# A gated feed-forward kernel: split value units in one PSUM bank in place of two, more of them, and row folds that add across the columns first

## The chip, the cores and the metric

The kernel runs on one core of a Trainium2 chip. The metric is the device time of one execution in microseconds (us). PSUM is the memory that matmuls write to; it is used here in 8 banks. Engine names: PE is the matmul engine (TensorE), PEld its weight loads, DVE is VectorE, ACT is ScalarE, POOL is GpSimd, SP issues DMAs. A profile shows one execution; its span is 1 to 3 us shorter than the time that is measured around it.

## The reference, cut to what matters

```python
def _attn_ref(x):                      # x: (8, 3008, 256)
    X = np.fft.fft(x, axis=1)
    X = np.fft.fft(X, axis=2)
    return X.real.astype(np.float32)

def _moe_ref(x, w_gate, w_val, w_out): # x: (24064, 256), d_ff 1536
    g = x @ w_gate
    silu = g * (1.0 / (1.0 + np.exp(-g)))
    val = x @ w_val
    return (silu * val @ w_out).astype(np.float32)
```

The kernel uses the symmetry of the transform. For each pair of output rows k and M-k it computes an even part P and an odd part Q. A row's value (or gate) is "even + odd", the mirrored row's is "even - odd". So one column of a tile serves two rows, called plus and minus below.

## The kernel before

Work goes through 24 tiles of at most 512 columns. A tile has 12 units, one for each 128 of the 1536 hidden features. A unit makes gate and value for plus and minus rows, and the two products `hp` and `hm`. Between the units run the output matmuls of the tile before (four at a time, 256 columns each), the row transforms of later rows (`L567`, `L543`), and on POOL the "folds", which prepare the coefficients of those transforms from the rows.

A plain unit needs six matmuls of 512 columns: plus gate (2), plus value (2), and one more on each to turn plus into minus. A split unit needs five: it takes the even and the odd part of the value apart, and DVE makes both combinations.

```python
psG = ...tile_pool(name="psG", bufs=3, PSUM)   # gate banks
psV = ...tile_pool(name="psV", bufs=3, PSUM)   # value banks
psO = ...tile_pool(name="psO", bufs=2, PSUM)   # output banks; 8 banks in all
...
SPLIT = (0, 2, 3, 5, 7, 9)                     # split units of a tile
SPLIT_END = (0, 1, 2, 4, 5, 7, 8, 10, 11)      # of the last two split tiles

def part_a(u):
    ...
    mm(g, Wp, 0, Pt, True, False)              # L716: all of mm()
    mm(g, Wq, 0, Qt, False, True)
    if split(u):
        e = psV.tile(...); mm(e, Wp, 1, Pt, True, True)     # even part, a bank
        o = psV.tile(...); mm(o, Wm, 1, Qt, True, True)     # odd part (times -2), another bank
        sg = Silu(g)                                        # ACT, L728
        es = bc[t] * w0[f] + e                              # DVE, L731
        vp = o * -0.5 + es                                  # DVE, L733
        vm[reversed] = o * 0.5 + es                         # DVE, L735
        hp[:, f] = sg * vp                                  # POOL, L736
        state[u] = (g, vm); return
    v = psV.tile(...); mm(v, Wp, 1, Pt, True, False); mm(v, Wq, 1, Qt, False, True)
    sg = Silu(g); hp[:, f] = sg * v                         # ACT L743, DVE L744
    state[u] = (g, v)

def part_b(u):                                 # one unit later
    g += Wm, Qt                                             # L753; for a plain unit v += Wm, Qt too
    if split(u):
        sg[reversed] = Silu(g); hm[:, f] = sg * v           # ACT L757, POOL L758
        return
    sg = Silu(g); hm[:, f][reversed] = sg * v               # ACT L761, DVE L762

# a fold, per 4 x 256 block of rows (on POOL)
tt(SDf[0], up, down, add); tt(SDf[1], up, down, subtract)   # L153, 1024 elements each
even: E = SDf[0] mirrored + SDf[0];  odd: O = SDf[1] mirrored - SDf[1]     # 512 each
...

for i, u in enumerate(units):                  # main loop, cut
    part_a(u); output matmuls x4; part_b(previous); output matmuls x4
    fold steps; row transforms in some units (after the fifth unit of a tile)
```

The code above is shortened (cuts are marked, calls are written as formulas). Tiles 0 to 2 and the last have no split units.

## Time and profile before

| | before |
|---|---|
| time, median of 4 | 688.56 us (687.79 to 689.6) |
| span of the profile | 685.5 us |
| PE, DVE, ACT, POOL busy | 672.8, 514.6, 432.9, 579.1 us |
| matmuls | 4374 |

The first two parts of the page below, and its chain, are of the kernel before: busy time of each engine with the share of the span and the number of instructions, then the chain of work that ended last.

```profile
PE 672.8 (98%) x4374; PEld 414.2 (60%) x4374; DVE 514.6 (75%) x919; ACT 432.9 (63%) x764; POOL 579.1 (84%) x565
...
PE 89%; DVE 5%; issue 2%; POOL 2%; ACT 0%; DVEq 0%; ACTq 0%; POOLq 0%
```

PE is the limit. The windows view of the kernel before says so for the main part; columns are the window, its length, busy time and number of instructions of PE, PEld, DVE, ACT and POOL, then clock, DMA share and GB/s.

```profile
250.00:350.00 100.00, 99.63 (x645) 61.09 (x643) 77.31 (x132) 63.78 (x111) 98.42 (x90) 1.00 0.30 81
350.00:450.00 100.00, 99.62 (x639) 59.74 (x637) 75.50 (x132) 62.69 (x110) 94.65 (x89) 1.00 0.23 59
```

POOL is nearly as busy as PE here.

The timeline of the kernel before shows that: start, duration, engine, line, operation. Units f=2 and f=3 of one tile, both split (some lines left out):

```profile
248.35 0.38 PE L716 MATMUL g<-Pt,Wp 128*128 128x512 bf16 x1
248.56 0.38 PE L716 MATMUL g<-Qt,Wq 128*128 128x512 bf16 x1
248.78 0.38 PE L716 MATMUL v<-Pt,Wp 128*128 128x512 bf16 x1
249.00 0.38 PE L716 MATMUL v<-Qt,Wm 128*128 128x512 bf16 x1
...
249.20 0.75 DVE L731 SCALAR_TENSOR_TENSOR es<-bc,w,v 128x512 f32<-128x512 f32 x1 [0.73 <-PE v L716]
...
250.68 0.68 DVE L735 SCALAR_TENSOR_TENSOR vv<-v,es 128x512 f32<-128x512 f32 x1
...
250.95 0.38 PE L716 MATMUL v<-Pt,Wp 128*128 128x512 bf16 x1
...
251.28 0.68 DVE L762 TENSOR_TENSOR hm<-sg,v 128x512 bf16<-128x512 f32 x1
...
251.42 0.38 PE L716 MATMUL v<-Qt,Wm 128*128 128x512 bf16 x1
251.64 0.60 PE L676 MATMUL o<-Wo,hp 128*128 128x256 bf16 x4
```

In the first unit matmuls of 512 columns start 0.21 to 0.22 us apart: that is what one costs when nothing waits. In the second, the odd part's matmul starts 0.47 us after the even part's, 0.26 us late. It starts 0.06 us after DVE has ended its read of the older odd part (250.68 + 0.68 = 251.36): it waits for the bank.

From the starts of all matmuls one can work out a "gap": the time to the next start, less columns/2.4 + 2.5 ns (215.8 ns for 512 columns, which fits undisturbed neighbours to about 1 ns). Summed over the run, matmuls at this price need 645.0 us, and the gaps after 25 us that matter are: 7.57 us before the value matmuls of units after 60 us (0.26 us each in most cases), and 13.22 us in the row transforms after 60 us.

### The profile page before, as it was taken

The page shows a single profiled execution, that of the slowest core. Times are in us where ns is not written, and L with a number is a line of the kernel's source. Part 1 is how long each engine was busy: PE and PEld are TensorE (multiplying, and loading weights), DVE is VectorE, ACT ScalarE, POOL GpSimd, SP SyncE. Part 2 cuts the span into 40 slices and gives each one's busy share as a digit, 9 for nine tenths or more (in the row PEclk, how much of TensorE's full clock was granted, in tenths as well). Part 3 has the DMA queues.
Part 4 walks back from the last instruction along what each step waited for, and adds up shares of the span by engine and source line. Part 5 has one row for each costly group of instructions (what it writes and reads, how often), then busy time and mean ns, then how long its engine had stood idle before and what let it go on. Part 6 is the DMA issues. An engine that isn't in the chain of part 4 may idle for free.

```text
span 685.5 us, 13259 instructions
## 1 busy us (share of the span) xinstructions
PE 672.8 (98%) x4374; PEld 414.2 (60%) x4374; DVE 514.6 (75%) x919; ACT 432.9 (63%) x764; POOL 579.1 (84%) x565
## 2 busy tenths in 40 slices
PE   8999999999999999999999999999999999999997
PEld 5446655666656566565665566655665656656676
DVE  8896667777777777777777777777786777788862
ACT  7676655666656666565666666655665656656663
POOL 8897987899998999999998989997999555658920
PEclk9999999999999999999999999999999999999999
DMA  9657353324315213335134111125111111101112
GB/s 220 115 77 133 102 138 113 96 76 101 99 32 134 67 51 105 86 71 131 41 76 116 48 32 47 47 58 128 46 48 32 38 40 33 47 31 47 47 48 70
DMA packets 45567, 52.55 MB, mean 77 GB/s; under 512 B 6290, under 2 KB 33466, under 8 KB 45498
## 3 DMA queue, kind: packets, MB, share of 16 engines
q1 hardware_dynamic: 42314, 49.35, 27.4%
q0 software_dynamic: 3184, 2.36, 2.7%
q8 instruction: 34, 0.56, 0.4%
q14 instruction: 35, 0.29, 0.2%
HBM read 29.39 MB, written 24.65 MB: 79 GB/s over the span
## 4 chain that ended last, share of the span: by engine, by line
PE 89%; DVE 5%; issue 2%; POOL 2%; ACT 0%; DVEq 0%; ACTq 0%; POOLq 0%
PE o L676 34%; PE v L716 17%; PE g L716 16%; PE g L753 9%; PE v L753 4%; PE g L567 3%; PE v L567 3%; DVE vv L735 3%; DVE vv L733 1%; PE v L543 1%; PE g L543 1%; PE g L856 1%; PE g L421 1%; PE v L421 1%; PE o L430 0%
## 5 line engine op out<-in xcount | busy, mean ns | idle before, releaser
L736 POOL TENSOR_TENSOR hp<-sgv,vv 128x512 bf16<-128x512 f32 (+1 forms) x126 | 160.1, 1272 | 54.3 <-DVE vv L733 42.4
L676 PE MATMUL o<-Wo,hp 128*128 128x256 bf16 (+2 forms) x1140 | 169.7, 273 | 0.0
L676 PE MATMUL o<-Wo,hm 128*128 128x256 bf16 (+2 forms) x1140 | 169.7, 273 | 0.0
L758 POOL TENSOR_TENSOR hm<-sgv,vv 128x512 bf16<-128x512 f32 (+1 forms) x126 | 159.6, 1272 | 8.5 <-ACT sgv L757 8.1
L676 PEld LDWEIGHTS <-hp 128*128 128x128 bf16 (+2 forms) x1140 | 111.9, 98 | 68.3 <-issue 7.8
L676 PEld LDWEIGHTS <-hm 128*128 128x128 bf16 (+2 forms) x1140 | 111.8, 98 | 64.8 <-issue 4.9
L744 DVE TENSOR_TENSOR hp<-sg,v 128x512 bf16<-128x512 f32 (+2 forms) x162 | 107.9, 666 | 33.2 <-ACT sg L743 32.4
L731 DVE SCALAR_TENSOR_TENSOR es<-bc,w,v 128x512 f32<-128x512 f32 (+1 forms) x126 | 93.7, 744 | 50.5 <-PE v L716 50.3
L762 DVE TENSOR_TENSOR hm<-sg,v 128x512 bf16<-128x512 f32 (+2 forms) x162 | 107.4, 663 | 24.1 <-ACT sg L761 14.4
L761 ACT ACTIVATE sg<-g 128x512 f32<-128x512 f32 (+2 forms) x162 | 94.7, 585 | 45.6 <-PE g L753 45.4
L743 ACT ACTIVATE sg<-g 128x512 f32<-128x512 f32 (+2 forms) x162 | 94.4, 583 | 45.0 <-PE g L716 43.5
L716 PE MATMUL g<-Qt,Wq 128*128 128x512 bf16 (+2 forms) x288 | 108.0, 375 | 0.5 <-DVE Qt L580 0.5
L716 PE MATMUL g<-Pt,Wp 128*128 128x512 bf16 (+2 forms) x288 | 108.1, 376 | 0.1
L716 PE MATMUL v<-Pt,Wp 128*128 128x512 bf16 (+2 forms) x288 | 108.0, 375 | 0.0
L753 PE MATMUL g<-Qt,Wm 128*128 128x512 bf16 (+2 forms) x288 | 108.0, 375 | 0.0
L757 ACT ACTIVATE sgv<-g 128x512 f32<-128x512 f32 (+1 forms) x126 | 75.3, 598 | 47.4 <-PE g L753 41.1
L728 ACT ACTIVATE sgv<-g 128x512 f32<-128x512 f32 (+1 forms) x126 | 75.1, 596 | 40.3 <-PE g L716 35.5
L733 DVE SCALAR_TENSOR_TENSOR vv<-v,es 128x512 f32<-128x512 f32 (+1 forms) x126 | 87.0, 690 | 17.6 <-PE v L753 1.0
L735 DVE SCALAR_TENSOR_TENSOR vv<-v,es 128x512 f32<-128x512 f32 (+1 forms) x126 | 85.7, 680 | 2.7 <-POOL hm L758 2.7
L716 PEld LDWEIGHTS <-Wp 128*128 128x128 bf16 x576 | 56.2, 98 | 41.0 <-issue 4.2
L682 ACT COPY ev<-o 128x512 f32<-128x512 f32 x90 | 52.7, 586 | 30.8 <-PE o L676 28.2
L153 POOL TENSOR_TENSOR SDf<-XA 128x1024 f32<-128x1024 f32 x28 | 66.0, 2364 | 5.2 <-DMA XC<-in_x_dram 3.3
(165 smaller groups left out, 738.0 us busy)
## 6 DMA issues: line engine op xcount, KB each, us to landing
out_dram<-ev SPq DMA_DIRECT2D x96, 128.0 KB
XA<-in_x_dram SPq DMA_DIRECT2D x32, 256.0 KB
XA<-in_x_dram SPq DMA_DIRECT2D x112, 64.0 KB
XC<-in_x_dram SPq DMA_DIRECT2D x32, 120.0 KB
XC<-in_x_dram SPq DMA_DIRECT2D x105, 32.0 KB
out_dram<-ev SPq DMA_DIRECT2D x12, 120.0 KB
out_dram<-ev SPq DMA_DIRECT2D x10, 112.0 KB
XA<-in_x_dram SPq DMA_DIRECT2D x1, 1024.0 KB
```

The costliest lines, as they stand in the source:

```text
L676: nc.tensor.matmul(ps[:n, j, :], hts[minus][:, f, c:c + n], Wo[:, f, :], start=(f == 0), stop=(f == nF - 1))
L716: nc.tensor.matmul(ps[:, :w], Wt[:, gv, fs], src[:, :w], start=start, stop=stop, skip_group_check=True)
L731: stt(es[:, :w], bc[t][:, :w], w0[:, f:f + 1], e[:, :w], op0=Alu.mult, op1=Alu.add)
L733: stt(vp[:, :w], o[:, :w], -0.5, es[:, :w], op0=Alu.mult, op1=Alu.add)
L735: stt(vm[:, w - 1::-1], o[:, :w], 0.5, es[:, :w], op0=Alu.mult, op1=Alu.add)
L736: nc.gpsimd.tensor_tensor(hts[t][0][:, f, :w], sg[:, :w], vp[:, :w], op=Alu.mult)
L743: nc.scalar.activation(sg[:, :w], g[:, :w], AF.Silu)
L744: nc.vector.tensor_tensor(hts[t][0][:, f, :w], sg[:, :w], v[:, :w], op=Alu.mult)
L753: nc.tensor.matmul(ps[:, :w], Wm[:, gv, f * P:(f + 1) * P], Qt[:, :w], start=False, stop=True, skip_group_check=True)
L758: nc.gpsimd.tensor_tensor(hts[t][1][:, f, :w], sg[:, :w], v[:, :w], op=Alu.mult)
L761: nc.scalar.activation(sg[:, :w], g[:, :w], AF.Silu)
L762: nc.vector.tensor_tensor(hts[t][1][:, f, w - 1::-1], sg[:, :w], v[:, :w], op=Alu.mult)
```

## The change

A split unit now starts its value with the even part alone in one bank. DVE reads it (`es`), and one unit later PE adds the odd part onto the same bank. Plus is then the bank itself, and minus is twice `es` less the bank. The plus product moves from POOL to DVE. There are more split units (8 of 12, in the last two split tiles 10). A fold adds one mirrored row block across the columns first, so that one sum of about 1024 elements takes the place of two.

```diff
-    SPLIT = (0, 2, 3, 5, 7, 9)
-    SPLIT_END = (0, 1, 2, 4, 5, 7, 8, 10, 11)
+    SPLIT = (0, 2, 3, 5, 6, 8, 9, 11)
+    SPLIT_END = (0, 1, 2, 3, 5, 6, 7, 8, 9, 11)
@@ part_a, split unit
-            e = psV.tile([P, T], F32, name="v")
-            mm(e, Wp, 1, Pt, True, True)
-            o = psV.tile([P, T], F32, name="v")
-            mm(o, Wm, 1, Qt, True, True)
...
+            v = psV.tile([P, T], F32, name="v")
+            mm(v, Wp, 1, Pt, True, False)
...            (silu of plus into sp, es as before from v)
-            stt(vp[:, :w], o[:, :w], -0.5, es[:, :w], op0=Alu.mult, op1=Alu.add)
-            stt(vm[:, w - 1::-1], o[:, :w], 0.5, es[:, :w], op0=Alu.mult, op1=Alu.add)
-            nc.gpsimd.tensor_tensor(hts[t][0][:, f, :w], sg[:, :w], vp[:, :w], op=Alu.mult)
+            state[u] = (g, v, sg, es)
@@ part_b, split unit
+            nc.tensor.matmul(v[:, :w], Wq[:, 1, fs], Qt[:, :w], start=False, stop=True, ...)
+            nc.vector.scalar_tensor_tensor(vm[:, w - 1::-1], es[:, :w], 2.0, v[:, :w],
+                                           op0=Alu.mult, op1=Alu.subtract)
+            nc.scalar.activation(sm[:, w - 1::-1], g[:, :w], AF.Silu)
+            nc.gpsimd.tensor_tensor(hts[t][1][:, f, :w], sm[:, :w], vm[:, :w], op=Alu.mult)
+            nc.vector.tensor_tensor(hts[t][0][:, f, :w], sp[:, :w], v[:, :w], op=Alu.mult)
@@ fold_steps
-            tt(SDf[r, a], X[r, 0:4, q, :], X[r, 7:3:-1, 1 - q, :], op=op)       # twice: add, subtract
+            tt(F[:, :, 1:D], up[:, :, 1:D], down[:, :, D - 1:0:-1], op=Alu.add) # once
+            tt(E[:, :, P:P + 1], up[:, :, 0:1], down[:, :, 0:1], op=Alu.add)    # 4 elements
...            (even and odd read F; 12 fold steps in place of 14; buffers: sp 3, sgv 3, es 3, vv 3)
```

Even with 38 more split units a split unit keeps its five matmuls, so only their number changes the count.

More of the change, by code (lines that the diff above doesn't have):

```diff
@@ L142, in load_c, with fold_steps, cross @@
                                      in_=rows_at(b, 0, [[R * D, 1], [R * D, 4], [1, D]]))])
-    def fold_steps(eng, X, CE, BB, q, r, given=None):
+    def fold_steps(eng, X, CE, BB, q, r):
         tt = eng.tensor_tensor
-        S, Dd = given or (SDf[r, 0], SDf[r, 1])
+        F = SDf[r, q]
         E, O = EOf[r, 0], EOf[r, 1]
-        def sd(a, op):
-            tt(SDf[r, a], X[r, 0:4, q, :], X[r, 7:3:-1, 1 - q, :], op=op)
+        up, down = X[r, 0:4, q], X[r, 7:3:-1, 1 - q]
+        def cross():
+            tt(F[:, :, 1:D], up[:, :, 1:D], down[:, :, D - 1:0:-1], op=Alu.add)
+            tt(E[:, :, P:P + 1], up[:, :, 0:1], down[:, :, 0:1], op=Alu.add)
         def even():
-            tt(E[:, :, 0:P], S[:, :, P:0:-1], S[:, :, P:D], op=Alu.add)
-            eng.tensor_copy(E[:, :, P:P + 1], S[:, :, 0:1])
+            tt(E[:, :, 0:P], F[:, :, P:0:-1], F[:, :, P:D], op=Alu.add)
         def odd():
-            tt(O[:, :, 0:P], Dd[:, :, P:0:-1], Dd[:, :, P:D], op=Alu.subtract)
+            tt(O[:, :, 0:P], F[:, :, P:0:-1], F[:, :, P:D], op=Alu.subtract)
         def ab():
@@ L169, in bb, with quarter_rows @@
         def bb():
-            tt(BB[r, q, 0], E[:, 0:4:3, 0:P], E[:, 2:0:-1, 0:P], op=Alu.subtract)
-            tt(BB[r, q, 1], O[:, 0:2, 0:P], O[:, 2:4, 0:P], op=Alu.subtract)
-            tt(BB[r, q, 1, :, 0:1], S[:, 3::-3, 0:1], S[:, 1:3, 0:1], op=Alu.subtract)
-        return [lambda: sd(0, Alu.add), lambda: sd(1, Alu.subtract), even, odd, ab, ce, bb]
+            quarter_rows(tt, E, O, BB[r, q])
+        return [cross, even, odd, ab, ce, bb]
+    def quarter_rows(tt, E, O, B_):
+        tt(B_[:, 0], E[:, 0:4:3, 0:P], E[:, 2:0:-1, 0:P], op=Alu.subtract)
+        tt(B_[:, 1], O[:, 0:2, 0:P], O[:, 2:4, 0:P], op=Alu.subtract)
+        tt(B_[:, 1, :, 0:1], E[:, 3::-3, P:P + 1], E[:, 1:3, P:P + 1], op=Alu.subtract)
     coefA, coefC = {}, {}
@@ L490 @@
     for q in range(2):
-        steps = fold_steps(nc.gpsimd, None, CEa, BBa, q, slice(0, P),
-                           given=(SA[:, 0, :, q, :], SA[:, 1, :, q, :]))
-        for i in (2, 3, 6):
-            steps[i]()
+        S, Dd = SA[:, 0, :, q, :], SA[:, 1, :, q, :]
+        E, O = EOf[:, 0], EOf[:, 1]
+        ptt(E[:, :, 0:P], S[:, :, P:0:-1], S[:, :, P:D], op=Alu.add)
+        nc.gpsimd.tensor_copy(E[:, :, P:P + 1], S[:, :, 0:1])
+        ptt(O[:, :, 0:P], Dd[:, :, P:0:-1], Dd[:, :, P:D], op=Alu.subtract)
+        quarter_rows(ptt, E, O, BBa[:, q])
     nc.gpsimd.dma_start(out=Wo, in_=moe_w_out.rearrange("(f p) d -> p f d", p=P))
@@ L616 @@
     sgp = ctx.enter_context(tc.tile_pool(name="sg", bufs=3))
-    sgv = ctx.enter_context(tc.tile_pool(name="sgv", bufs=4))
-    esp = ctx.enter_context(tc.tile_pool(name="es", bufs=2))
+    spp = ctx.enter_context(tc.tile_pool(name="sp", bufs=3))
+    sgv = ctx.enter_context(tc.tile_pool(name="sgv", bufs=3))
+    esp = ctx.enter_context(tc.tile_pool(name="es", bufs=3))
     bcp = ctx.enter_context(tc.tile_pool(name="bc", bufs=2))
-    vvp = ctx.enter_context(tc.tile_pool(name="vv", bufs=4))
+    vvp = ctx.enter_context(tc.tile_pool(name="vv", bufs=3))
     evp = ctx.enter_context(tc.tile_pool(name="evO", bufs=4))
@@ L722, in part_a @@
         if split(u):
-            e = psV.tile([P, T], F32, name="v")
-            mm(e, Wp, 1, Pt, True, True)
-            o = psV.tile([P, T], F32, name="v")
-            mm(o, Wm, 1, Qt, True, True)
-            sg = sgv.tile([P, T], F32, name="sgv")
+            v = psV.tile([P, T], F32, name="v")
+            mm(v, Wp, 1, Pt, True, False)
+            sg = spp.tile([P, T], F32, name="sp")
             nc.scalar.activation(sg[:, :w], g[:, :w], AF.Silu)
-            stt = nc.vector.scalar_tensor_tensor
             es = esp.tile([P, T], F32, name="es")
-            stt(es[:, :w], bc[t][:, :w], w0[:, f:f + 1], e[:, :w], op0=Alu.mult, op1=Alu.add)
-            vp = vvp.tile([P, T], F32, name="vv")
-            stt(vp[:, :w], o[:, :w], -0.5, es[:, :w], op0=Alu.mult, op1=Alu.add)
-            vm = vvp.tile([P, T], F32, name="vv")
-            stt(vm[:, w - 1::-1], o[:, :w], 0.5, es[:, :w], op0=Alu.mult, op1=Alu.add)
-            nc.gpsimd.tensor_tensor(hts[t][0][:, f, :w], sg[:, :w], vp[:, :w], op=Alu.mult)
-            state[u] = (g, vm)
+            nc.vector.scalar_tensor_tensor(es[:, :w], bc[t][:, :w], w0[:, f:f + 1], v[:, :w],
+                                           op0=Alu.mult, op1=Alu.add)
+            state[u] = (g, v, sg, es)
             return
@@ L750, in part_b @@
         Pt, Qt = pq_tiles(t)
-        g, v = state.pop(u)
-        for gv, ps in ((0, g), (1, v))[:1 if split(u) else 2]:
-            nc.tensor.matmul(ps[:, :w], Wm[:, gv, f * P:(f + 1) * P], Qt[:, :w], start=False, stop=True,
-                             skip_group_check=True)
-        if split(u):
-            sg = sgv.tile([P, T], F32, name="sgv")
-            nc.scalar.activation(sg[:, w - 1::-1], g[:, :w], AF.Silu)
-            nc.gpsimd.tensor_tensor(hts[t][1][:, f, :w], sg[:, :w], v[:, :w], op=Alu.mult)
+        g, v, *kept = state.pop(u)
+        fs = slice(f * P, (f + 1) * P)
+        nc.tensor.matmul(g[:, :w], Wm[:, 0, fs], Qt[:, :w], start=False, stop=True, skip_group_check=True)
+        if kept:
+            nc.tensor.matmul(v[:, :w], Wq[:, 1, fs], Qt[:, :w], start=False, stop=True, skip_group_check=True)
+            sp, es = kept
+            vm = vvp.tile([P, T], F32, name="vv")
+            nc.vector.scalar_tensor_tensor(vm[:, w - 1::-1], es[:, :w], 2.0, v[:, :w],
+                                           op0=Alu.mult, op1=Alu.subtract)
+            sm = sgv.tile([P, T], F32, name="sgv")
+            nc.scalar.activation(sm[:, w - 1::-1], g[:, :w], AF.Silu)
+            nc.gpsimd.tensor_tensor(hts[t][1][:, f, :w], sm[:, :w], vm[:, :w], op=Alu.mult)
+            nc.vector.tensor_tensor(hts[t][0][:, f, :w], sp[:, :w], v[:, :w], op=Alu.mult)
             return
+        nc.tensor.matmul(v[:, :w], Wm[:, 1, fs], Qt[:, :w], start=False, stop=True, skip_group_check=True)
         sg = sgp.tile([P, T], F32, name="sg")
@@ L771, in spread @@
         seq.extend((lo + (i * (hi - lo)) // (n - 1), what, i) for i in range(n))
-    spread(("C", 1), 14, 6, 14)
-    spread(("A", 1), 14, 15, 24)
+    spread(("C", 1), 12, 6, 14)
+    spread(("A", 1), 12, 15, 24)
     lo = 25
@@ L777 @@
         u = slot[(b, 0)] - 1
-        spread(("C", b), 14, lo, (lo + u) // 2)
-        spread(("A", b), 14, (lo + u) // 2 + 1, u)
+        spread(("C", b), 12, lo, (lo + u) // 2)
+        spread(("A", b), 12, (lo + u) // 2 + 1, u)
         lo = min(u + 26, slot[(b + 1, 0)] - 2)
-        spread(("A", b + 1), 14, u + 2, lo)
+        spread(("A", b + 1), 12, u + 2, lo)
         lo += 1
@@ L792, in fold_step @@
         kind, b = what
-        q, j = divmod(i, 7)
+        q, j = divmod(i, 6)
         if i == 0:
@@ L801, in fold_step @@
         queue[what].pop(0)()
-        if q == 1 and j == 1:
+        if q == 1 and j == 0:
             act_at.setdefault(max(unit + 2, 11), []).append(what)
```

## The prediction

> **What bounds the kernel.** TensorE. In the windows view it is busy 99.5 to 99.7% of the stretches from 150 to 550 us; DVE has 76%, POOL 84 to 98%. But busy time overstates a matmul: the groups give 375 ns for 512 columns, while in the PE timeline of an undisturbed stretch they start 0.215 us apart (300.27, 300.49, 300.70, 300.92), and the 256-column output matmuls 0.109 us. The Trainium skill says the same ("TensorE: Matmul & The Clock Gate", Back-to-back issue gap: columns/2.4 + 2.5 ns when warm). At this price all matmuls need 645 us of the 685.5 us span. About 36 us are extra gap: 13 us before 60 us, about 12 us in the row transforms, and 7.5 us at one place, the second value matmul of split units (v<-Qt,Wm after v<-Pt,Wp): 0.26 us whenever the unit before was split too (f=3; f=1, 8, 11 in the last split tiles), 0.05 us at f=0. Even and odd part hold two of three value banks, and DVE has not finished reading the older pair.
>
> **What the change does.**
> 1. Split units go from 18 tiles x 6 + 2 x 9 = 126 to 18 x 8 + 2 x 10 = 164. A split unit has 5 matmuls, another 6, before and after: 38 fewer (the instruction order agrees). 38 x 0.2155 = 8.2 us off the critical engine, not 38 x 0.375 = 14 us.
> 2. A split unit takes one value bank; v(u) waits only for the reads of v(u-3), even between neighbouring split units. The 7.5 us should nearly vanish.
> 3. DVE per split unit: es, one subtraction, one product, 0.744 + 0.69 + 0.67 = 2.1 us, as before. Another unit costs 1.33. 38 x 0.78 = +30 us: about 540 us, 80%, still under PE.
> 4. POOL: 252 products of 1.27 us become 164 (-112 us); two 2.36 us row sums of a fold become one (about -50 us): 579 to about 420 us. POOL is 2% of the chain, and DVE's products last the same with POOL busy or idle, so this gains almost nothing.
> 5. New cost: the row transforms follow f=4, and their second value bank was that of f=3, now a split unit whose DVE reads end late: estimate 0.1 us each, plus up to 1 us in the last split tiles, where five split units stand in a row and DVE needs as long as PE (5 x 0.2155 + 8 x 0.109 = 1.95 us a unit).
>
> **Sum.** 688.45 - 8.2 - 7.5 + about 1.5 = 674.3 us; all of it is PE's path. 80% range 670.5 to 680. About -2.0%, on the border: faster by over 2% 0.50, within 2% 0.48, slower 0.02.
>
> **What would show it.** Gap before the value matmuls of split units from 7.5 us to under 1 us; PE matmuls 4374 to 4336; DVE near 540, POOL near 420, ACT unchanged at 433; nothing changes before 80 us and in the tail.
>
> **What would make it wrong.** If DVE falls behind (split pairs, the burst of sums after a transform), PE waits for a value bank, or for es before it may add the odd part: the gain is 3 to 5 us smaller. Likewise if the transforms' new bank wait is 0.5 us. If POOL's products held PE where I read issue, the gain is larger.

## More of the kernel before

The groups of the kernel before (busy us and mean ns of one, then idle time before them and what ended it):

```profile
L736 POOL TENSOR_TENSOR hp<-sgv,vv 128x512 bf16<-128x512 f32 (+1 forms) x126 | 160.1, 1272 | 54.3 <-DVE vv L733 42.4 <-ACT sg L761 11.9
L758 POOL TENSOR_TENSOR hm<-sgv,vv 128x512 bf16<-128x512 f32 (+1 forms) x126 | 159.6, 1272 | 8.5 <-ACT sgv L757 8.1 <-DVE hp L744 0.4
L731 DVE SCALAR_TENSOR_TENSOR es<-bc,w,v 128x512 f32<-128x512 f32 (+1 forms) x126 | 93.7, 744 | 50.5 <-PE v L716 50.3
L733 DVE SCALAR_TENSOR_TENSOR vv<-v,es 128x512 f32<-128x512 f32 (+1 forms) x126 | 87.0, 690 | 17.6 <-PE v L753 1.0 <-POOL hp L736 0.3
L735 DVE SCALAR_TENSOR_TENSOR vv<-v,es 128x512 f32<-128x512 f32 (+1 forms) x126 | 85.7, 680 | 2.7 <-POOL hm L758 2.7
L153 POOL TENSOR_TENSOR SDf<-XA 128x1024 f32<-128x1024 f32 x28 | 66.0, 2364 | 5.2 <-DMA XC<-in_x_dram 3.3 <-DMA out_dram<-ev 1.3 <-DMA XA<-in_x_dram 0.5
...
L716 PE MATMUL v<-Qt,Wm 128*128 128x512 bf16 (+1 forms) x126 | 47.6, 378 | 2.6 <-DVE vv L735 0.4
```

The last line hides the main point. It gives 378 ns for a matmul and 2.6 us of idle time over 126 of them. Both mislead, because a matmul's record (0.38 us) is longer than the time after which the next may start.

## The result and the profile after

| | before | changed |
|---|---|---|
| time, median | 688.56 us | 671.88 us (671.68 to 672.59) |
| ratio | | 0.9763, interval 0.9749 to 0.9777 |
| time in a second group of runs | 687.49 us | 673.07 us, ratio 0.9788 (0.9775 to 0.9801) |

A ratio is the mean time of one kernel's runs over the mean of the other's of the same rounds, so it is not quite the ratio of the medians quoted.

The same parts of the changed kernel's page:

```profile
PE 656.5 (98%) x4269; PEld 411.6 (61%) x4336; DVE 549.4 (82%) x957; ACT 433.5 (65%) x764; POOL 423.8 (63%) x455
...
PE 94%; DVE 2%; DMA 2%; issue 1%; POOL 1%; ACT 0%; DVEq 0%; ACTq 0%; POOLq 0%
```

There are 4336 weight loads, the 38 fewer that were expected. The 4269 matmuls are a defect of this trace: 67 records are missing, nearly all of the second gate matmul (223 of 288). In a second trace of the same kernel all 4336 are there; I use that one wherever gaps are counted.

Windows of the changed kernel (first trace):

```profile
250.00:350.00 100.00, 99.34 (x645) 62.32 (x655) 85.89 (x143) 65.86 (x115) 73.26 (x73) 1.00 0.36 90
350.00:450.00 100.00, 99.40 (x638) 60.91 (x647) 85.27 (x144) 64.40 (x113) 68.14 (x68) 1.00 0.20 56
```

PE is as full as before (99.97% in the first of these windows in the second, complete trace), DVE went from 77 to 86%, POOL from 98 to 73%. Groups of the changed kernel:

```profile
L762 POOL TENSOR_TENSOR hm<-sgv,vv 128x512 bf16<-128x512 f32 (+1 forms) x164 | 208.3, 1271 | 190.2 <-DVE vv L758 180.9 <-ACT sgv L761 8.9
L735 DVE SCALAR_TENSOR_TENSOR es<-bc,w,v 128x512 f32<-128x512 f32 (+1 forms) x164 | 121.8, 743 | 5.9 <-PE v L723 5.1 <-ACT sp L733 0.6 <-ACT bc L865 0.2
L758 DVE SCALAR_TENSOR_TENSOR vv<-es,v 128x512 f32<-128x512 f32 (+1 forms) x164 | 112.6, 686 | 13.7 <-PE v L755 10.3 <-POOL BBa L178 0.6 <-POOL BBc L178 0.2
L763 DVE TENSOR_TENSOR hp<-sp,v 128x512 bf16<-128x512 f32 (+1 forms) x164 | 111.3, 679 | 0.0
L154 POOL TENSOR_TENSOR SDf<-XA 128x1020 f32<-128x1020 f32 x14 | 32.9, 2350 | 11.5 <-DMA XC<-in_x_dram 7.8 <-DMA XA<-in_x_dram 3.5
```

The three DVE operations of a split unit last 743, 686 and 679 ns, together 2.11 us, as the old three did (744, 690, 680). POOL has idle time again (190 us before its product), and the large fold sums are half as many.

Two neighbouring split units of the changed kernel, in the timeline of the second trace:

```profile
602.50 0.38 PE L723 MATMUL v<-Pt,Wp 128*128 128x512 bf16 x1
...
603.15 0.38 PE L753 MATMUL g<-Qt,Wm 128*128 128x512 bf16 x1
603.37 0.38 PE L755 MATMUL v<-Qt,Wq 128*128 128x512 bf16 x1
...
604.02 0.38 PE L723 MATMUL g<-Pt,Wp 128*128 128x512 bf16 x1
604.24 0.38 PE L723 MATMUL g<-Qt,Wq 128*128 128x512 bf16 x1
604.45 0.38 PE L723 MATMUL v<-Pt,Wp 128*128 128x512 bf16 x1
604.47 0.68 DVE L763 TENSOR_TENSOR hp<-sp,v 128x512 bf16<-128x512 f32 x1
604.66 0.60 PE L683 MATMUL o<-Wo,hm 128*128 128x256 bf16 x4
```

No matmul is late: 604.02, 604.24, 604.45, 604.66. DVE reads the older unit's bank (604.47 on) while PE goes on in another. Over the whole second trace the gap before value matmuls is 0.01 us (7.57 before). A clean account is the time from the start of the first unit to the start of the last: 646.02 us before, 630.53 us changed, a difference of 15.49 us. What lies outside, mainly the start, varies from run to run: the first unit started at 25.19 us in the trace before, and at 26.02 and 26.42 us in the two of the changed kernel. In the first of them a weight load of PE waits 1.2 us for a DMA; the chain follows that DMA back for 10 us, which is its "DMA 2%".

### The profile page after: what moved, and what is told of

Its sections match the earlier page's. It is cut to its first block, busy times and chain, and to the rows that moved or that the text cites. A ratio compares the mean times of both kernels' runs of the same rounds, so it can differ in the third digit from the quotient of the medians. Undisturbed runs are those within 1.5% of the kernel's fastest.

```text
span 670.8 us, 12888 instructions
## 1 busy us (share of the span) xinstructions
PE 656.5 (98%) x4269; PEld 411.6 (61%) x4336; DVE 549.4 (82%) x957; ACT 433.5 (65%) x764; POOL 423.8 (63%) x455
## 4 chain that ended last, share of the span: by engine, by line
PE 94%; DVE 2%; DMA 2%; issue 1%; POOL 1%; ACT 0%; DVEq 0%; ACTq 0%; POOLq 0%
PE o L683 37%; PE g L723 16%; PE v L723 14%; PE g L753 9%; PE v L755 5%; PE v L765 4%; PE g L573 3%; PE v L573 3%; DMA W<-in_moe_w_val_dram 2%; PE g L862 1%; PE v L549 1%; PE g L549 1%; PE o L434 1%; DVE hp L744 0%; DVE hm L768 0%
## 5 line engine op out<-in xcount | busy, mean ns | idle before, releaser
L762 POOL TENSOR_TENSOR hm<-sgv,vv 128x512 bf16<-128x512 f32 (+1 forms) x164 | 208.3, 1271 | 190.2 <-DVE vv L758 180.9
L733 ACT ACTIVATE sp<-g 128x512 f32<-128x512 f32 (+1 forms) x164 | 98.0, 597 | 73.6 <-PE g L723 48.6
L735 DVE SCALAR_TENSOR_TENSOR es<-bc,w,v 128x512 f32<-128x512 f32 (+1 forms) x164 | 121.8, 743 | 5.9 <-PE v L723 5.1
L758 DVE SCALAR_TENSOR_TENSOR vv<-es,v 128x512 f32<-128x512 f32 (+1 forms) x164 | 112.6, 686 | 13.7 <-PE v L755 10.3
L761 ACT ACTIVATE sgv<-g 128x512 f32<-128x512 f32 (+1 forms) x164 | 98.2, 599 | 39.1 <-PE g L753 39.1
L763 DVE TENSOR_TENSOR hp<-sp,v 128x512 bf16<-128x512 f32 (+1 forms) x164 | 111.3, 679 | 0.0
L744 DVE TENSOR_TENSOR hp<-sg,v 128x512 bf16<-128x512 f32 (+2 forms) x124 | 82.4, 664 | 26.6 <-ACT sg L743 24.8
L743 ACT ACTIVATE sg<-g 128x512 f32<-128x512 f32 (+2 forms) x124 | 71.9, 580 | 36.1 <-PE g L723 26.9
L767 ACT ACTIVATE sg<-g 128x512 f32<-128x512 f32 (+2 forms) x124 | 71.9, 580 | 32.5 <-PE g L753 32.3
L755 PE MATMUL v<-Qt,Wq 128*128 128x512 bf16 (+1 forms) x164 | 62.1, 378 | 0.0
L723 PEld LDWEIGHTS <-Wq 128*128 128x128 bf16 x412 | 40.3, 98 | 19.9 <-issue 0.3
```

Source lines behind the costliest of these rows:

```text
L723: nc.tensor.matmul(ps[:, :w], Wt[:, gv, fs], src[:, :w], start=start, stop=stop, skip_group_check=True)
L733: nc.scalar.activation(sg[:, :w], g[:, :w], AF.Silu)
L735: nc.vector.scalar_tensor_tensor(es[:, :w], bc[t][:, :w], w0[:, f:f + 1], v[:, :w], op0=Alu.mult, op1=Alu.add)
L744: nc.vector.tensor_tensor(hts[t][0][:, f, :w], sg[:, :w], v[:, :w], op=Alu.mult)
L755: nc.tensor.matmul(v[:, :w], Wq[:, 1, fs], Qt[:, :w], start=False, stop=True, skip_group_check=True)
L758: nc.vector.scalar_tensor_tensor(vm[:, w - 1::-1], es[:, :w], 2.0, v[:, :w], op0=Alu.mult, op1=Alu.subtract)
```

## The experiments

All are timed beside the kernel before on the same chip; all gave correct results.

| run | time, us | before, us | ratio (95%) | first to last unit, us |
|---|---|---|---|---|
| new folds only | 687.66 | 688.12 | 0.9992 (0.9979 to 1.0006) | 645.89 |
| one bank, 126 split units, old folds | 681.13 | 688.12 | 0.9897 (0.9884 to 0.9911) | 638.79 |
| two banks, odd part later | 683.01 | 688.12 | 0.9924 (0.9912 to 0.9936) | 640.39 |
| two banks, 164 split units | 745.82 | 688.12 | 1.0837 (1.0822 to 1.0852) | 703.76 |
| the same with new folds | 716.89 | 688.42 | 1.0417 (1.0397 to 1.0438) | 674.65 |
| changed, old folds | 672.19 | 688.42 | 0.9773 (0.9757 to 0.9788) | 630.58 |
| changed, 10 of 12 split | 665.11 | 688.42 | 0.9667 (0.9651 to 0.9683) | 622.79 |
| changed, all 12 split | 656.71 | 688.42 | 0.9547 (0.9532 to 0.9563) | 614.96 |
| all 12 split, old folds | 674.39 | 687.49 | 0.9808 (0.9788 to 0.9829) | 631.01 |
| all 12 split, third tile too | 661.61 | 687.49 | 0.9629 (0.9606 to 0.9651) | 617.84 |
| the same, folds begun later | 660.99 | 687.33 | 0.9616 (0.9598 to 0.9634) | 617.94 |

My theory: the time comes from PE, 38 matmuls and the waits for a value bank. The rival: POOL, 97% busy for 300 us before, had been holding something, and its relief (155 us less) gives part of the gain.

### Each part alone

New folds only: `fold_steps`, its callers and its 12 steps are taken from the changed kernel, everything else from before.

> The kernel before with only the new row folds (POOL's two 2.36 us sums become one). Theory (TensorE path: fewer matmuls and no wait for a value bank): no change, within 0.3% of 688.5 us, POOL busy down by about 50 us to about 530, gap before the second value matmul of split units still about 7.5 us. Rival (part of the gain is POOL's relief): a third of the gain, about 5 us, so about 683 us.

Measured: 687.66 us, no change within 0.2%. POOL fell to 530.0 us, and the gap before value matmuls stayed at 7.51 us. Fifty microseconds less on an engine that is nearly full bought nothing.

One bank only: the changed kernel with the old folds and

```diff
-    SPLIT = (0, 2, 3, 5, 6, 8, 9, 11)
-    SPLIT_END = (0, 1, 2, 3, 5, 6, 7, 8, 9, 11)
+    SPLIT = (0, 2, 3, 5, 7, 9)
+    SPLIT_END = (0, 1, 2, 4, 5, 7, 8, 10, 11)
```

This carries the move of the plus product to DVE and the new buffer counts with it; neither is tested apart.

> The changed kernel with the old folds and the old 126 split units: only the one value bank, and with it the plus product on DVE in place of POOL. Theory: the 7.5 us of bank waits go and nothing else, less about 0.5 us at the row transforms: 681.5 us (680.5 to 682.5), matmuls stay 4374. Rival: with POOL at about 420 us instead of 579, the gain is most of the whole change's 16.7 us, below 678 us.

Measured: 681.13 us with all 4374 matmuls. From first to last unit it is 7.23 us shorter than before; the gap before value matmuls is 0.00 us and that in the row transforms rose from 13.22 to 13.60 us. POOL has 427.7 us to do here, hardly more than in the whole change, and the gain stops at the bank waits.

### The wait taken away without touching POOL

The kernel before, with the odd part's matmul issued after the first four output matmuls:

```diff
-            o = psV.tile([P, T], F32, name="v")          # in part_a
-            mm(o, Wm, 1, Qt, True, True)
...
         part_a(u)
         if owork:
             owork.run(4)
+        part_o(u)      # o, vp, vm and the plus product, moved here unchanged
```

> The kernel before, two value banks and POOL as before, but the odd part's matmul of a split unit is issued after the first group of four output matmuls (0.44 us later), when its bank is free. Theory: the bank waits go without any change of POOL or of the number of operations: 681.5 us (680.5 to 683). Rival (POOL's relief): 688 us, no change.

Measured: 683.01 us, 1% faster, at POOL's old load of 579.3 us. The gap before value matmuls fell from 7.57 to 0.19 us. The whole gain did not come: the row transforms' gaps rose by 1.59 us, to 14.81, so from first to last unit it saves 5.63 us. In its trace the added gaps lie in three of the transforms: PE waits there for POOL's coefficients (at 170 and 308 us), or for DVE, which waits for a product of POOL (at 281 us). This rules POOL's load out as the source of the 7 us of bank waits: moving one matmul 0.44 us later in the queue, with POOL's work as before, removes them. But it also shows how near POOL stood.

### More split units in two banks

Only the two lists of the change are put into the kernel before.

> The kernel before with 164 split units (the new lists) and nothing else. Matmuls alone would give -8.2 us, bank waits of 0.26 us for some 40 more neighbouring pairs +10 us. But POOL needs 76 more products of 1.27 us: 579 + 97 = 676 us, and all of it between 20 and 660 us. Theory: POOL becomes the limit, 695 to 715 us, POOL busy over 95% of the main part. Rival (POOL does not hold the time in this range): 686 to 692 us.

Measured: 745.82 us, 8% slower, and worse than I expected. The windows view, and three lines of the wait view (who waited for whom: us in total, times, longest us), of this run:

```profile
250.00:350.00 100.00, 86.58 (x530) 50.82 (x528) 68.83 (x118) 53.16 (x93) 99.69 (x93) 0.97 0.27 73
```

```profile
PE v L716 <- DVE vv L735: 28.8, 31, 2.4
...
DVE vv L735 <- POOL hm L758: 21.4, 22, 2.0
...
PE o L676 <- POOL hp L736: 17.6, 15, 3.4
```

POOL is 99.7% busy, PE only 86.6%. POOL's products come late, DVE then has no buffer for the next value, so it reads the banks late, so PE waits for a bank; and the output matmuls wait for POOL's products directly. One reason why my figure was too low is that I added up POOL's total work, 676 us (671.0 measured), as if it could be spread evenly. It can't: POOL has nothing to do in the last 28 us of this run, and from 550 to 650 us, when the folds are done, it has 15 us idle.

The same with the new folds:

> The kernel that took 745.8 us (two value banks, 164 split units) with the new row folds. Theory (POOL limits it: 98.9 to 99.7% busy from 150 to 550 us there): POOL has 50 us less to do, so most of that comes off: 698 to 715 us, still slower than before. Rival (it is limited by the waits for the value banks, 43.9 us of gap, whatever POOL does): 735 us or more.

Measured: 716.89 us, 29 us less, just outside my range and far from the rival's. POOL is still 96 to 99% busy from 150 to 550 us, and the gap before the odd part's matmul fell from 43.9 to 30.8 us, so what the bank waits alone would cost at 164 split units is not measured. POOL's 50 us less are worth 29 us here and nothing in the kernel before. So POOL was not the limit before, but it stood right behind: the count of split units could not be raised without first taking work from POOL, and the change does that by moving the plus product to DVE.

### What the folds are for

The changed kernel with the old folds:

> The changed kernel with the old row folds (two POOL sums of 2.36 us each again); the 164 split units in one value bank stay. Theory: with one bank POOL has room (424 us + 50 = about 474 us busy), so the folds give nothing here: the same as the changed kernel, ratio to before 0.976 within 0.002, about 672 us. Rival (the folds gave a share): 676 us or more.

Measured: 672.19 us, ratio 0.9773 against 0.9763 and 0.9788 for the changed kernel itself; POOL at 474.0 us. At 164 split units the folds add nothing.

### How many split units the new form carries

The changed kernel with other lists: `SPLIT = (0, 1, 2, 3, 5, 6, 7, 8, 9, 11)`, then all twelve.

> The changed kernel with 10 of 12 units split in every tile from the fourth on (200 split units in place of 164). 36 matmuls fewer, 36 x 0.2155 = 7.8 us: 664 us if DVE keeps up (663 to 667). DVE gets 36 x 0.78 = 28 us more, 577 us busy, about 92% in the main part, against 85.7% in the changed kernel; POOL +46 us, about 470. Rival (DVE is already the limit in a run of split units, its 2.1 us against PE's 1.95 us): 668 us or more, with PE waits on DVE.

> All 12 units split (240). 76 matmuls fewer than the changed kernel, 16.4 us: 655.5 us if PE stayed the limit. But DVE gets 59 us more, 608 us, nearly all of the main part: I expect DVE to become the limit, 657 to 666 us, DVE over 95% busy in the main part and PE waiting for DVE before the value matmuls.

Measured: 665.11 and 656.71 us. From first to last unit the former is 7.74 us shorter than the changed kernel, for 36 matmuls (7.8 us expected). The latter is shorter by another 7.83 us, for 40 matmuls (8.6 us); the 0.8 us between lie in short waits before the first gate matmul of a unit, whose gaps rose by 0.77 us. I had expected DVE to become the limit with all units split; it did not. The windows view and DVE's timeline of that run:

```profile
250.00:350.00 100.00, 99.96 (x657) 61.96 (x656) 95.91 (x162) 67.24 (x118) 94.98 (x92) 1.00 0.38 99
```

```profile
246.17 0.69 DVE L758 SCALAR_TENSOR_TENSOR vv<-es,v 128x512 f32<-128x512 f32 x1
246.77 0.68 DVE L763 TENSOR_TENSOR hp<-sp,v 128x512 bf16<-128x512 f32 x1
247.37 0.74 DVE L735 SCALAR_TENSOR_TENSOR es<-bc,w,v 128x512 f32<-128x512 f32 x1
248.12 0.69 DVE L758 SCALAR_TENSOR_TENSOR vv<-es,v 128x512 f32<-128x512 f32 x1
```

DVE is 96% busy, yet PE is at 99.96%. The records of DVE's operations overlap: 0.69, 0.68 and 0.74 us long, they start 0.60, 0.60 and 0.75 us apart, 1.95 us for a unit in place of the 2.11 that their durations add up to. That is just PE's pace for a split unit (five matmuls of 0.216 and eight of 0.109 us). The last of the three distances, 0.75 us (also the median over the run), holds a short wait: in most of these cases `L758` starts 0.115 us after the end of the matmul record (`L755`) that it needs. Where it starts later than that, DVE is catching up, and the distance is mostly 0.65 to 0.66 us. So a unit costs DVE about 0.60 + 0.60 + 0.65 = 1.85 us, and some 5% were still left.

POOL, at 95%, has hardly more. All twelve split with the old folds:

> All 12 units split in one bank (656.7 us with the new folds), with the old folds. POOL was 94 to 95% busy from 150 to 350 us there; the old folds add 50 us over the run, some 9 us to each 100 us of that stretch, over 100%. Theory (the folds matter only where POOL is full): slower than with the new folds by 5 us or more, 662 to 675 us, PE waiting for POOL's products. Rival (POOL has reserve through its queues and buffers): 656 to 658 us.

Measured: 674.39 us (671.98 to 676.16), 17.7 us slower than with the new folds. Its windows and waits:

```profile
250.00:350.00 100.00, 94.68 (x597) 57.28 (x595) 87.52 (x149) 60.17 (x107) 97.40 (x89) 0.97 0.29 79
```

```profile
ACT sgv L755 <- POOL hm L756: 30.6, 33, 2.5
...
DVE vv L752 <- POOL hm L756: 13.1, 20, 1.6
```

ACT and DVE wait for POOL to give buffers back, and PE (94.7%) waits for them. Of the one-bank kernels that were run with both folds (164 and 240 split units), only this one gains from the new folds.

### Splitting one tile more

The third tile was left whole by all kernels so far. The edit is `2 <= u[0]` in place of `3 <= u[0]` in `split`, with all twelve split.

> All 12 units split, and in the third tile too, which was left whole: 12 matmuls fewer, 2.6 us: 654.1 us if nothing waits there (between 80 and 100 us DVE is at 64%, POOL at 62%). If it changes nothing or loses, the early stretch has another limit.

Measured: 661.61 us with a wide spread (659.1 to 663.72), slower than without it. The timeline of this run has one long stop:

```profile
89.31 2.34 POOL L154 TENSOR_TENSOR SDf<-XC 128x1020 f32<-128x1020 f32 x1 [5.46 <-DMA XC<-in_x_dram]
...
91.76 1.26 POOL L762 TENSOR_TENSOR hm<-sgv,vv 128x512 bf16<-128x512 f32 x1
...
93.06 0.60 ACT L761 ACTIVATE sgv<-g 128x512 f32<-128x512 f32 x1 [5.93 <-POOL hm L762]
...
93.70 0.59 PE L723 MATMUL g<-Pt,Wp 128*128 128x512 bf16 x1 [3.74 <-ACT sgv L761]
```

POOL stands 5.46 us at a fold whose rows have not landed. The products behind it in the queue wait too, then ACT for their buffer, then PE for a gate bank. In the run with the third tile whole, POOL waited 7.23 us at this fold, but no product stood behind it. To test this, the folds of that block begin nine units later (`lo = 34` in place of `lo = 25`):

> The kernel that took 661.6 us (all units split from the third tile on), with the folds of the third batch's remainder rows starting at unit 34 in place of unit 25. In that run POOL stood 5.46 us on such a fold until its rows had landed (89.3 us), the minus products stood behind it in POOL's queue, and PE then stood 3.74 us waiting for an activation that waited for a product. Theory: without that stop, 12 matmuls fewer than the 656.7 us kernel: 654 us (653 to 656), and no PE wait at 90 us. Rival (DVE or POOL as such has no room there): 659 us or more.

Measured: 660.99 us. The stop is gone: that tile takes 26.96 us in place of 32.17 (29.48 when it is not split; this trace lacks 67 matmul records, but none of those that begin a unit). But the delayed folds are now squeezed into fewer units, and the gain is given back: the fifth and sixth tile take 25.57 and 30.31 us, against 23.66 and 26.97 in the run that took 656.71 us, with PE waits of up to 1.95 us at 155 us. So the cause of the stop is shown, and this remedy does not help. The best version is the changed kernel with all twelve units split, without the third tile: 656.71 us, 4.5% below before (ratio of the same rounds) and 2.3 to 2.4% below the changed kernel (medians of different groups).

### The changed kernel again

> The changed kernel unaltered, timed beside the others of this group. From the first to the last unit its trace is 15.5 us shorter than before's (8.2 us of matmuls, 7.2 us of waits). If the 16.7 us between the medians holds more than scatter, it should show again: theory 688.4 - 15.5 = 672.9 us within 1 us; rival (another 1 us or more comes from somewhere else): 671.5 us or less.

Measured: 673.07 us, ratio 0.9788, 14.6 us by the mean of the runs; the first group gave 0.9763, 16.3 us. The 15.5 us between first and last unit lie between them. The surplus of the first group did not come again, so I put it down to scatter between groups; no run shows another cause. By the second group's interval (up to 0.9801) the change lies on the border of 2%, as the prediction had it.

## Why the prediction was right or wrong

It was right in size and in its two causes; the time came in 2.4 us below its centre and inside its range. One term was mis-sized, and the rule for which units wait was too wide.

- Matmuls: 38 x 0.2155 = 8.2 us foretold. Between the one-bank kernel with 126 split units and the changed kernel the distance from first to last unit falls by 638.79 - 630.53 = 8.26 us. Pricing them by the mean duration in the groups (375 ns, 14 us) would have foretold 6 us too much. The section on the gap that the prediction cites also has a smaller figure for a stream of matmuls, which does not fit (see the last section). The Trainium skill, "Perfetto Trace Analysis", section Identifying the Most-Contended Engine, warns that matmul busy time is no good measure of how close a kernel is to its roofline; here it hid 7.5 us of waits and overstated the price of a matmul.
- Bank waits: 7.5 us foretold to vanish; 7.57 us went to 0.01, and the one-bank kernel alone is 7.23 us shorter. The prediction said that a unit waits "whenever the unit before was split too" and that the older pair's reads hold the banks. The trace shows waits in 24 of 29 such neighbours, all of them after a plain unit. In all 24 the odd part's matmul starts 0.05 us after `L735` ends, while DVE reads the plain unit's value for another 0.5 us, and the older even part was read 1.4 us before or earlier. So the third bank is the plain unit's. Where three split units stand in a row, the matmul starts 0.2 to 0.7 us before `L735` ends. The remedy works for either, since a split unit takes one bank less. The rival, POOL's relief, falls by three runs: the folds alone gave 0.1% (not significant), the moved matmul took the waits away with POOL as loaded as ever, and the old folds put back cost nothing.
- New cost: this is the term that was mis-sized. I allowed about 1.5 us (0.1 us for each row transform, and up to 1 us in the last split tiles). Measured: the transforms' gaps rose by 0.38 us, 0.07 to 0.08 us at five of the 14 after 60 us (one matmul starts 0.19 us late in place of 0.10) and next to nothing at the others; in the last split tiles nothing was lost. The step that failed was "DVE needs as long as PE" there: 2.1 us is the sum of durations, but the all-split kernel shows DVE doing a unit in 1.85 us when it is behind, against PE's 1.95.
- The other 1.3 us of the miss are not explained by any mechanism: the second group of runs gave 673.07 us.
- DVE: 540 us foretold, 549.4 measured. The sum of the durations rose by 27.7 us (559.1 to 586.8, second trace), near the 30 foretold; busy time, which counts overlapped stretches once, rose by more, since the overlap of its operations fell from 44.5 to 37.3 us.
- POOL: 420 us foretold, 423.8 measured, and "gains almost nothing" holds for the kernel as it stood. What the prediction did not say is why the change needs it: with two banks the 164 split units cost 58 us more than before. With POOL nearly full all the time, 50 us less of its work took off 29 of them; how the rest divides between POOL and the waits for banks stays open.

## What to carry to other kernels

Price an operation on a pipelined engine by the distance of starts in an undisturbed stretch, not by its duration; look for waits in the same way, since overlapping records hide those shorter than the overlap. When an operation of two results holds two buffers of a pool of three, ask whether the second can be added onto the first after the first has been read: it halves the buffers, and here it cost 0.4 us. Look at what holds each buffer of the pool before you name the culprit. An engine that was 97% busy and off the critical path gave nothing when it was relieved, but it decided how far the next step could go: measure the step without the relief, and the relief without the step.

## What the Trainium skill lacked or had wrong

- "TensorE: Matmul & The Clock Gate", Back-to-back issue gap: it gives two figures for 512 columns, about 216 ns for the isolated gap and about 131 ns for a sustained stream of weight load and matmul pairs. This kernel is such a stream, and undisturbed matmuls of 512 columns start 215 to 216 ns apart; the smaller figure would have made the 38 matmuls worth 5.0 us, and 8.26 were measured.
- "Perfetto Trace Analysis", Identifying the Most-Contended Engine: it advises, beside the share of peak FLOP/s, the busy share of weight loads as a measure of the matmul engine's headroom. Here the latter is 61% in the main part of the kernel before and 62% with all units split, where the engine starts matmuls with hardly a gap, so here it does not show that no headroom is left. That page does not mention that overlapping records also hide waits (0.26 us each, 7.6 us in all, of which the wait view shows 0.4).
- "Perfetto Trace Analysis", Optimizing Scalar/DVE Operations: it says that part of a DVE operation's recorded latency, the write acknowledgement, overlaps with the next. The traces agree as to the overlap: 0.68 and 0.69 us long, 0.60 us apart. It does not draw the consequence: durations that add up to 2.11 us fit into 1.85 us, so they can't be added up to tell whether DVE keeps pace.
- "GPSIMD Engine Reference", Specifications: it says that POOL and DVE share SBUF interfaces, with contention for DVE instructions with two SBUF inputs or in a 2-port mode. `vv` (`L733` of the kernel before) reads one operand from PSUM and one from SBUF, and no contention shows: it lasts 692 ns whether POOL is busy or idle during it. So this is no fault of the page: its limit to those cases is not contradicted, and DVE operations with two SBUF inputs were not compared.
